# A planner that counts the overlap of VectorE and ScalarE instructions, and three more long score stretches

## The chip, the cores and the metric

One core of one Trainium2 chip. The metric is the time of one execution in device microseconds (us), lower is better; every median below comes with its range and number of runs. The span of a profile is 1.7 to 2.1 us shorter than the time of the same run; I compare spans with spans and times with times.

## The reference, cut to what matters

```python
def reference(q, k, v, w_gate, w1, w2):               # q, k, v: (4, 8, 768, 64)
    attn = _attn_ref(q, k, v)                         # window of +-15 keys, and 24 block summaries
    x = attn.transpose(0, 2, 1, 3).reshape(3072, 512)
    return _moe_ref(x, w_gate, w1, w2)                # 8 experts, 512 -> 1024 -> 512, Sinkhorn routing

# in _attn_ref: k_sum = max of k over blocks of 32 keys (summaries of keys)
#               scores = local scores (banded) and q . k_sum; one softmax over both
```

The kernel works on 16 "pairs" of heads (0 to 15). Expert 0 runs as filler work between the pairs, up to some 165 us; the other seven experts follow, and they fill TensorE (busy for 475.00 us of the 475 from 165 to 640 us).

## The kernel before

The kernel doesn't issue instructions in the order of its source. It adds *units* (an engine, a planned cost in us, what it depends on, the buffers it opens or uses) to a plan, and `Plan.order` simulates the engines greedily: it takes the unit that can start first, sets its planned start and end, and so on. The order that comes out is the order in which the kernel issues each engine's instructions. No time is measured in this; the planned costs are numbers in the source. One line in `order`:

```python
class Plan:
    HOP = 0.15                          # planned hand-over between engines
    ...
    def order(self):
        ...                             # t = when operands, buffers and the engine are free
            u.start, u.end, u.on = t, end, e
            free[e] = end               # the engine is free when the unit ends
```

```python
    X_BY_DMA = 12
    WHOLE = 10
    ...
        def key_max(i):                                  # a VectorE unit of one instruction
            nc.vector.tensor_reduce(out=ks[r][:, 0, 0:24], in_=kT[r][:]..., axis=AX.X, op=ALU.max)

        def key_max_split(i):                            # "the split": ksT, one small instruction
            nc.vector.tensor_tensor(out=ksT[r][:, 64:128]..., in0=ks[r][:]..., in1=own[:]..., op=ALU.mult)

        def summaries_2(i):                              # TensorE: ss needs ksT
            r, ss = i % NB, bank("a", "ss")
            for h in range(2):
                nc.tensor.matmul(ss[:, 0:HS], lhsT=ksT[r][:, 64 - 64 * h:192 - 64 * h], rhs=qT[r]..., ...)

        def block_out(i):                                # two instructions, the second reads the first
            nc.vector.tensor_tensor(out=dst..., in0=vs, in1=own_n..., op=ALU.mult)
            if i >= PB:
                nc.vector.tensor_copy(out=ve[0:64, 1:G, :], in_=ve[0:64, 0:1, :]...)

        def edges(i):                                    # four instructions
            for j in range(2):
                q0 = 64 + 32 * j
                nc.vector.tensor_tensor(out=ee[q0:q0 + 32, ...], in0=er[0:32, ...], in1=band[0:32, ...], op=ALU.mult)
                nc.vector.tensor_tensor(out=ee[q0:q0 + 32, ...], in0=er[96:128, ...], in1=band[96:128, ...], op=ALU.mult)

        def pair_whole(i, prio):                         # pairs 4 to 15
            ...
            bufs = [Buffer("s")] + (2 * [None] if i < WHOLE else [Buffer("a"), Buffer("a")])
            U["S", i, 0] = U["S", i, 1] = add("PE", 0.4 if i < WHOLE else 0.6, lambda: scores(i), deps, prio, ...)
            U["X", i, 0] = add("ACT", 0.97, lambda: score_exp(i, 0), [U["S", i, 0]], prio, uses=bufs[:1])
            if i < WHOLE:                                # two stretches of six score matmuls
                U["S", i, 1] = add("PE", 0.4, lambda: scores_1(i), deps, prio, opens=[buf])
            ...                                          # else one of twelve, in one double and two single banks
            U["ed", i] = add("DVE", 0.78, lambda: edges(i), ...)
            ...
        # block_out of pairs 4 to 15 is planned with 0.7
```

The softmax here doesn't subtract the row's maximum and nothing guards it: scores larger than these inputs give would overflow.

## Time and profile before

| kernel before | |
|---|---|
| time | 666.17 us, median of 3 (666.14 to 666.85); with the runs made beside the change 666.27, 6 runs (665.79 to 667.65) |
| span of the profile | 664.1 us (a run of 665.77 us), TensorE busy 99% |
| VectorE, ScalarE busy | 83%, 62% |
| excess on TensorE | 16.0 us, of which 7.7 between 20 and 165 us |

"Excess" is the time from one matmul's start to the next one's, less the median of its shape, summed. It shows waits that a list of idle times hides, because a matmul row lasts longer than the time to the next start (379 against 216 ns at 512 columns in the trace of before).

```profile
71.76 1.46 PE L211 MATMUL hps<-xT,w 128*128 128x384 f16 x8
73.06 0.49 PE L461 MATMUL ss<-qT,ksT 128*128 128x384 bf16 x2
```

The split ends at 72.22 + 0.21 = 72.43 and ss starts at 73.06, so 0.63 us of filler (hps) lie between. Over the twelve pairs 4 to 15 this distance is 0.35 us at the least: before the change TensorE never waited for a split.

### The profile page before, as it was taken

Reading aid. Unit: us, or ns where it says so; the run is one execution under the profiler, and the core shown is the slowest. Engines: PE = TensorE matmul, PEld = TensorE weight load, DVE = VectorE, ACT = ScalarE, POOL = GpSimd, SP = SyncE. Lnnn points to the kernel's source line nnn. Section 1 sums busy time; section 2 is a strip of 40 time slices with the busy share of each in tenths; the row PEclk is TensorE's granted clock in tenths of the full one; section 3 lists DMA queues with packets and bytes.
Section 4 is the critical chain, followed back from the end, with each engine's and each line's share of the span. In section 5 each row is a group of like instructions: output and inputs, shape, how many; then the busy total and the mean of one; then the engine's idle time right before and its main releaser. Section 6 shows DMA issues by size and latency. Waiting matters only on the chain.

```text
span 664.1 us, 13257 instructions
## 1 busy us (share of the span) xinstructions
PE 656.6 (99%) x5131; PEld 435.9 (66%) x5132; DVE 550.1 (83%) x1036; ACT 410.9 (62%) x769; POOL 199.0 (30%) x257
## 2 busy tenths in 40 slices
PE   8999999999999999999999999999999999999997
PEld 4666666545766666666666666666666666666666
DVE  7899897799988887887779877988778877988776
ACT  6677676556885566556665665555655656556652
POOL 8899522100132222212322222223122213222123
PEclk9999999999999999999999999999999999999999
DMA  9999932700953747373754665373838465335656
GB/s 167 181 145 145 143 70 43 128 1 2 157 96 65 126 75 118 64 128 65 110 97 71 121 91 101 64 127 65 127 64 135 73 96 96 64 64 112 157 134 202
DMA packets 112558, 67.89 MB, mean 102 GB/s; under 512 B 77936, under 2 KB 90480, under 8 KB 112496
## 3 DMA queue, kind: packets, MB, share of 16 engines
q0 software_dynamic: 94816, 57.46, 64.9%
q1 hardware_dynamic: 17152, 9.58, 5.9%
q8 instruction: 40, 0.66, 0.4%
q14 instruction: 22, 0.18, 0.1%
q10 hardware_dynamic: 528, 0.02, 0.0%
HBM read 52.45 MB, written 6.29 MB: 88 GB/s over the span
## 4 chain that ended last, share of the span: by engine, by line
PE 96%; DVE 3%; DMA 1%; issue 0%; ACT 0%; POOLq 0%; DVEq 0%
PE yps L815 22%; PE pA L764 22%; PE pY L815 17%; PE pQ L764 11%; PE hps L211 6%; PE yps L216 6%; PE pR L764 5%; PE sg L347 1%; DMA qst<-in_q_dram 1%; PE av L512 1%; PE vs L357 1%; PE tkq L303 1%; PE av L435 1%; DVE xs L543 1%; PE ss L461 1%; PE av L441 1%
## 5 line engine op out<-in xcount | busy, mean ns | idle before, releaser
L815 PEld LDWEIGHTS <-h 128*128 128x128 f16 x2352 | 230.1, 98 | 88.5 <-issue 1.0
L843 POOL DMA_DIRECT2D out_acc<-y x120 | 101.7, 891 | 372.1 <-ACT y L839 110.3
L839 ACT ACTIVATE y<-pY,P_sb 128x256 f32<-128x256 f32 x168 | 79.8, 477 | 123.3 <-PE pY L815 121.6
L830 DVE SCALAR_TENSOR_TENSOR out_acc<-yps,P_sb,out_acc 128x512 f32<-128x512 f32 x128 | 95.1, 744 | 29.0 <-PE yps L815 29.0
L798 DVE TENSOR_TENSOR h<-h 128x1024 f16<-128x1024 f16 x168 | 109.3, 683 | 1.4
L815 PE MATMUL pY<-w,h 128*128 128x256 f16 x672 | 100.0, 273 | 0.6 <-ACT y L839 0.6
L815 PE MATMUL yps<-w2sum,h 128*128 128x256 f16 x672 | 98.4, 273 | 0.0
L764 PE MATMUL pA<-xT,w 128*128 128x512 f16 x336 | 98.3, 379 | 0.0
L815 PE MATMUL yps<-w,h 128*128 128x256 f16 x672 | 93.3, 273 | 0.0
L830 DVE SCALAR_TENSOR_TENSOR out_acc<-pY,P_sb,out_acc 128x512 f32<-128x512 f32 x84 | 62.8, 748 | 29.1 <-PE pY L815 27.4
L764 PEld LDWEIGHTS <-w 128*128 128x128 f16 x672 | 65.8, 98 | 31.6 <-issue 0.2
L764 PEld LDWEIGHTS <-w1sum 128*128 128x128 f16 x504 | 49.3, 98 | 45.0
L786 DVE CUSTOM_DVE_ANT_0 h<-pQ,snap 128x512 f16<-128x512 f32 x84 | 57.6, 685 | 7.0 <-ACT snap L207 4.3
L786 DVE CUSTOM_DVE_ANT_0 h<-pA,snap 128x512 f16<-128x512 f32 x84 | 57.3, 682 | 4.8 <-PE pA L764 4.8
L202 ACT ACTIVATE h<-pA 128x512 f16<-128x512 f32 x84 | 50.6, 603 | 12.6 <-PE pA L764 12.4
L202 ACT ACTIVATE h<-pR 128x512 f16<-128x512 f32 x84 | 50.1, 596 | 8.0 <-PE pR L764 7.7
L207 ACT COPY pR<-pA 128x512 f32<-128x512 f32 x83 | 47.5, 572 | 7.7 <-PE pA L764 6.9
L815 PE MATMUL pY<-w2sum,h 128*128 128x256 f16 x336 | 50.4, 273 | 0.0
L764 PE MATMUL pA<-xsum,w 128*128 128x512 f16 x168 | 50.0, 379 | 0.0
L764 PE MATMUL pR<-xT,w 128*128 128x512 f16 x168 | 50.0, 379 | 0.0
L764 PE MATMUL pQ<-xsum,w1sum 128*128 128x512 f16 x168 | 50.0, 379 | 0.0
L764 PE MATMUL pA<-xsum,w1sum 128*128 128x512 f16 x168 | 50.0, 379 | 0.0
(150 smaller groups left out, 854.3 us busy)
## 6 DMA issues: line engine op xcount, KB each, us to landing
out_acc<-y POOLq DMA_DIRECT2D x120, 256.0 KB, 3.4
w<-in_moe_w_dram POOLq DMA_DIRECT2D x14, 1024.0 KB, 10.7
out_dram<-out_acc SPq DMA_DIRECT2D x24, 256.0 KB, 2.4
qst<-in_q_dram POOLq DMA_DIRECT2D x32, 96.0 KB, 5.3
vx<-in_v_dram POOLq DMA_DIRECT2D x15, 192.0 KB, 6.2
kst<-in_k_dram POOLq DMA_DIRECT2D x24, 96.0 KB, 5.6
w<-in_moe_w_dram POOLq DMA_DIRECT2D x4, 256.0 KB, 7.6
w<-in_moe_w_dram POOLq DMA_DIRECT2D x2, 512.0 KB, 7.7
```

The costliest lines, as they stand in the source:

```text
L202: nc.scalar.activation(out=out, in_=in_, func=AF.Relu, bias=0.0, scale=1.0)
L207: (nc.scalar.copy if eng == "ACT" else nc.vector.tensor_copy)(out=out, in_=in_)
L211: nc.tensor.matmul(hp[:, 0:n], lhsT=w1s[e][:, dk, f * 128:(f + 1) * 128], rhs=xT[:, dk, t0:t0 + n], start=(dk == 0), stop=(dk == KD - 1))
L216: nc.tensor.matmul(yp[:, d], lhsT=h[:, f, c * 128:(c + 1) * 128], rhs=w2s[e][:, f, d], start=(f == 0), stop=(f == KF - 1))
L303: nc.tensor.transpose(t[:, g * 128:(g + 1) * 128], st[:, g, :, :].rearrange("p j d -> p (j d)"), ident)
L764: nc.tensor.matmul(dst[:], lhsT=lhsT, rhs=rhs, start=first and k == 0, stop=k == HK - 1, skip_group_check=True)
L786: nc.vector._custom_dve(dve_ops.TENSOR_ADD_SAT, out=ring(e, p, q)[:, q % 2, blk, :], in0=at[src, e, p, q][:], in1=at.pop(("snap", n, e, p, ...
L798: nc.vector.tensor_tensor(out=h[:, :, out_, :], in0=h[:, :, a, :], in1=h[:, :, b, :], op=op)
L815: nc.tensor.matmul(dst[:, d], lhsT=lhsT, rhs=rhs, start=f == 0 and n in (1, 5, 2), stop=f == HF - 1, skip_group_check=True)
L830: nc.vector.scalar_tensor_tensor(out=o, in0=y, scalar=scalar, in1=o, op0=ALU.mult, op1=ALU.add)
L839: nc.scalar.activation(out=at[key][:, d], in_=src, func=AF.Copy, bias=0.0, scale=P_sb[:, t, e:e + 1])
L843: nc.gpsimd.dma_start(out=o, in_=at.pop(("y", e, p, c, key))[:], accum_op=ALU.add)
```

## The change

Intent: where work is queued, a VectorE or ScalarE instruction often begins a little before the one in front of it ends (in the trace of before by 82 and 103 ns in the median, where it does), so let the planner free the engine that much earlier; and let pairs 5, 7 and 9 too run their scores in one stretch over all six key chunks, as pairs 10 to 15 did, to save changes between matmuls of 128 rows and of 64. Making `X_BY_DMA` a set changes nothing (pairs 12, 13, 14 in both). The Sinkhorn rows' planned cost goes from 1.65 to 1.5. The diff, cut:

```diff
     HOP = 0.15
+    OVERLAP = {"DVE": 0.07, "ACT": 0.09}
...
-            free[e] = end
+            free[e] = end - self.OVERLAP.get(e, 0.0)
...
-    X_BY_DMA = 12
-    WHOLE = 10
+    X_BY_DMA = {12, 13, 14}
+    WHOLE = {5, 7, 9, 10, 11, 12, 13, 14, 15}
...
-            if i >= WHOLE:
+            if i in WHOLE:
...                                   (the other tests of WHOLE and X_BY_DMA likewise)
-            rows = add("DVE", 1.65, sink_rows, prev, 0)
+            rows = add("DVE", 1.5, sink_rows, prev, 0)
```

More of the change, by code (lines that the diff above doesn't have):

```diff
@@ L384, in scores @@
             dst = [[sg[:, j, :] for j in range(2)], None]
-            if i >= WHOLE:
+            if i in WHOLE:
                 dst[1] = at["sg", i, 1] = [bank("a", "sg1") for _ in range(2)]
-            score_mms(i, dst, range(G if i >= WHOLE else HG))
+            score_mms(i, dst, range(G if i in WHOLE else HG))
         def scores_1(i):
@@ L948, in pair_whole @@
             deps = [U["kT", i, 0], U["kT", i, 1], U.get(("ed", i - 2))]
-            bufs = [Buffer("s")] + (2 * [None] if i < WHOLE else [Buffer("a"), Buffer("a")])
-            U["S", i, 0] = U["S", i, 1] = add("PE", 0.4 if i < WHOLE else 0.6, lambda: scores(i), deps, prio,
+            bufs = [Buffer("s")] + (2 * [None] if i not in WHOLE else [Buffer("a"), Buffer("a")])
+            U["S", i, 0] = U["S", i, 1] = add("PE", 0.4 if i not in WHOLE else 0.6, lambda: scores(i), deps, prio,
                                               opens=[x for x in bufs if x is not None])
             U["X", i, 0] = add("ACT", 0.97, lambda: score_exp(i, 0), [U["S", i, 0]], prio, uses=bufs[:1])
-            if i < WHOLE:
+            if i not in WHOLE:
                 buf = Buffer("s")
@@ L978, in pair_whole @@
                                     [U["A", i, h], U.get(("x", i - 2))], prio, uses=[buf])
-            if i >= X_BY_DMA and i % PB < PB - 1:
+            if i in X_BY_DMA:
                 U["xt", i] = add("SP", 1.5, lambda: x_dma(i), [U["no", i, 0], U["no", i, 1]], prio)
@@ L1100, in transposed @@
             nc.gpsimd.tensor_copy(out=warm[:, 1:2], in_=qT[r][0:32, W:W + 1])
-            if X_BY_DMA < NP:
+            if NP - 2 in X_BY_DMA:
                 nc.gpsimd.tensor_copy(out=warm[:, 4:5], in_=xT[0:32, PB - 2, (B - 1) * S:(B - 1) * S + 1])
@@ L1108 @@
         last[0] = add("POOL", 0.3, transposed, [last[0], U["near", NP - 1]] + [U["kT", NP - 1, z] for z in range(2)]
-                      + [U["x", i] for i in range(X_BY_DMA, NP - 1)])
+                      + [U["x", i] for i in X_BY_DMA])
         load("w1n", lambda: load_w1(1), 0.85, 5.0)
```

## The prediction

> **What bounds the kernel now.** I read the page's first part, then stretches, then TensorE's waits, then single starts in the timeline. The page:
>
> ```profile
> PE 656.6 (99%) x5131; PEld 435.9 (66%) x5132; DVE 550.1 (83%) x1036; ACT 410.9 (62%) x769; POOL 199.0 (30%) x257
> PE 96%; DVE 3%; DMA 1%; issue 0%; ACT 0%; POOLq 0%; DVEq 0%
> ```
>
> TensorE (PE) is busy for 99% of 664.1 us and holds 96% of the chain that ended last. VectorE (83%) and ScalarE (62%) have room. The change alters how the order of VectorE and ScalarE is planned, so the first question is whether TensorE waits for them at all. The busy time of two stretches, and all TensorE waits above 150 ns that the view of waits lists:
>
> ```profile
> 20.00:165.00 145.00, 144.83 (x1421) 88.08 (x1419) 126.64 (x317) 97.57 (x174) 67.99 (x96) 1.00 1.11 93
> 165.00:640.00 475.00, 475.00 (x3292) 321.92 (x3291) 391.62 (x606) 294.27 (x564) 107.71 (x128) 1.00 0.57 98
> PE idle L613 <- DVE zeros L632: 1.3, 1, 1.3
> PE tkq L312 <- DMA qst<-in_q_dram: 0.8, 1, 0.8
> PE pY L815 <- ACT y L839: 0.6, 1, 0.6
> PE tkq L300 <- ACT kst L207: 0.3, 1, 0.3
> ```
>
> The stretch columns are width, then busy time and count of PE, PEld, DVE, ACT and POOL. From 165 to 640 us (the seven Strassen experts) TensorE is busy all the time. The waits are three in the first 7 us and one at 658 us.
>
> A busy matmul row can hide a short wait, because a row is longer than the gap between starts: a 512-column row lasts 379 ns, but the median start-to-start is 216 ns. So I compared each start-to-start time with the median of its shape (216, 162, 109, 56 ns for 512, 384, 256, 128 columns; for rare shapes columns at the same rate) and called the rest excess. It sums to 16.0 us: 7.1 us before 20 us (start-up[...]), 7.7 us from 20 to 165, less than 0.2 us from 165 to 640, and 1.0 us after 640. Only the 7.7 and the 1.0 can be won by scheduling.
>
> Most of the 7.7 us is no wait for an engine. It is 93 to 97 ns at each place where TensorE passes between matmuls of 128 rows and of 64 (or 32):
>
> ```profile
> 63.70 1.02 PE L216 MATMUL yps<-w,h 128*128 128x512 f16 x4
> 64.66 0.38 PE L347 MATMUL sg<-qT,kT 64*128 64x160 bf16 x6
> 64.97 0.51 PE L550 MATMUL tx<-ident_x,xs 128*128 128x128 f16 x6
> ...
> 90.10 1.03 PE L216 MATMUL yps<-w,h 128*128 128x512 f16 x4
> 91.06 0.59 PE L347 MATMUL sg<-qT,kT 64*128 64x160 bf16 x12
> 91.58 1.04 PE L216 MATMUL yps<-w,h 128*128 128x512 f16 x4
> ```
>
> Columns: start, length, engine, line. Four 512-column matmuls take 4 x 0.216 = 0.864 us, so the stream is free at 63.70 + 0.864 = 64.56, yet the scores (sg, 64 rows) start at 64.66: 0.096 us lost on entry. The exit costs 92 to 93 ns in the same reckoning. A stretch of six score matmuls thus costs 0.096 + 0.31 (64.66 to 64.97) = 0.41 us, one of twelve 0.096 + 0.52 (91.06 to 91.58) = 0.62 us. Waits for data in 20 to 165 us that I can name are two: 0.285 us (a transpose waits for a normalization at 20.6) and 0.21 us (logits wait for xT at 66.2).
>
> [...]
>
> ```profile
> 647.52 0.83 ACT L839 ACTIVATE y<-pY,P_sb 128x256 f32<-128x256 f32 x2
> 657.05 1.41 DVE L830 SCALAR_TENSOR_TENSOR out_acc<-yps,P_sb,out_acc 128x512 f32<-128x512 f32 x2 [0.63 <-PE yps L815]
> ```
>
> Two ACTIVATEs of 477 ns (mean row of their group) take 0.83 us, so they overlap by 0.12; two 744 ns VectorE rows take 1.41, an overlap of 0.08. Over the whole trace the median overlap, where one row begins before the previous ends, is 82 ns on VectorE (467 cases) and 103 ns on ScalarE (197). The planner's new constants, 0.07 and 0.09 us, are therefore close and still cautious.
>
> **The change part by part.** No matmul is added or removed: both built programs have 5,124 matmuls of the same shapes.
>
> 1. Pairs 5, 7 and 9: two stretches of six score matmuls become one of twelve. Counted in the built programs, the changes of row tiling fall from 86 to 80 (three entries, three exits). 6 x 94.5 ns = 0.57 us less on TensorE. Cross-check: 3 x (2 x 0.41 - 0.62) = 0.60 us. TensorE is on the path, so I take **-0.57 us** in full.
>
> 2. The second half's exponential of these pairs comes in two pieces of 480 elements: 1.04 us for two against 0.97 for one of 960 (rows of this trace), 3 x 0.07 = 0.2 us more on ScalarE, which is 67% busy there: off the path, 0. The pieces hold two of three shared PSUM banks instead of one double bank. That is the price that could turn into waits.
>
> 3. The overlap in the planner. It changes no duration, only order and who does what. By the count of built instructions ScalarE loses 13 copies of snap from pA and 9 from pQ, and 2 seeds of pR, all to VectorE: 24 x about 0.69 us = 16.6 us. Against 391.6 us in the 475 us stretch VectorE goes from 82% to 86%, ScalarE by 24 x 0.57 = 13.7 us from 62% to 59%. TensorE has no excess there to give back, so the gain is 0 and only a loss is possible. I put **+0.1 us** on it.
>
> 4. Order in the attention part (20 to 165 us). To see whether new waits are likely I laid out both orders with the start-to-start times above and read how much TensorE work lies between a producer and its consumer. Transpose of q to scores: 1.39 us at the tightest before, 0.91 (pair 4) and 1.29 after. The copy between needs 0.17 (end of the transposes) + 0.55 on VectorE or 0.80 on ScalarE + about 0.1: 0.82 or 1.07 us. So pair 4 may wait some 0 to 0.2 us. First to second scores of a pair: 1.72 before, 1.54 after; an exponential needs about 0.17 + 0.97 + 0.1 = 1.24. Values to transposes of x: 1.30 and 1.32. Last transposes of batch 0 to its logits: some 1.9 us of work, where 0.21 us was waited. I expect **-0.2 us** from the two old waits and **+0.2 us** for new ones.
>
> 5. The planned 1.5 us for the Sinkhorn rows (1.65 before) changes no instruction. In the trace the four take about 1.6 us (131.55 to 133.16) beside expert work: 0.
>
> 6. Order of DMA: POOL's issues stand as before; on SyncE the near values of pair 10 now go before the transposes of pair 12, and those of pair 13 before the near values of pair 11. The transposes landed at 73 to 76 us, the scores of pair 12 start near 91 (84 before): far apart.
>
> 7. The end. TensorE's last 24 matmuls, with the group that waits for y at 658, and VectorE's last 20 instructions stand as before: 0.
>
> Sum: -0.57 + 0.1 - 0.2 + 0.2 = -0.47 us; 666.17 - 0.47 = 665.7. Since the new planner's picture of the two engines is nearer to the trace, I lean slightly to fewer waits and say **665.5 us**.
>
> **The rivals.**
> - VectorE becomes late in the expert stage. For: 24 more copies[...]. Against: 86% busy on an overstated count (overlaps of 82 ns), and TensorE waited nowhere before. If every tenth of the 24 made TensorE wait 0.3 us: about +0.7 us, 666.3.
> - The two shared banks held by scores make transposes, values or block sums wait. For: three banks serve all of these. Against: pairs 10 to 15 already run so, with excess between 70 and 140 us of 1.7 us, nearly all of it tiling changes. One wait of 0.5 us a pair: +1.5 us, 667.2.
> - A finer plan packs TensorE truly tighter, removing all named waits, 0.5 us, and the 0.3 us near 645: 664.8. Against: the order around 645 is unchanged, and waits beside switches are few.
>
> **Range and chances.** The most that scheduling could win is 0.57 + 0.5 + 0.3 = 1.4 us (0.2%). A loss beyond 2% would be 13 us, nearly twice all excess of the attention part, with no mechanism for it. The three timed runs spread over 0.7 us. Range 664.5 to 667.0; within 2% is almost certain.
>
> **What would show it.** Right: score stretches on TensorE 23 instead of 26, each entry still about 96 ns; 165 to 640 us filled, with no TensorE wait in the view of waits there; VectorE's busy time up by some 12 us over the whole span and ScalarE's down by some 10 (the 24 copies less some relus and copies of the attention part that go the other way), with the end moved by under 1.5 us. Wrong: a new TensorE row on VectorE or ScalarE in the list of waits (snap, kT/qT copies, er), or a start in 20 to 165 us that has moved later than the switches explain.

(What the trace of before shows of the start: the first 512-column matmuls begin 401 to 427 ns apart, up to 4.2 us, against 216 later. The "about 0.1" of part 4 is an estimate for two hand-overs; between 20 and 165 us of that trace a ScalarE or VectorE row that waited for TensorE begins 37 or 38 ns after the end of the row it waited for, in the median, and a matmul that waited for VectorE begins 0.05 us after it in the trace of the change, below.)

## More of the kernel before

The next lines are from the timeline of the kernel before (start in us, length, engine, line, operation, output and inputs, count): first VectorE, then TensorE. They show the split of pair 9 (the sixth of the twelve, as in the plan's order) and the summaries that need it.

```profile
72.22 0.21 DVE L341 TENSOR_TENSOR ksT<-ks,own 128x64 bf16<-128x64 bf16 x1
```

## The result, and the profile after

667.37 us, median of 6 (667.24 to 669.93), against 666.27 of the kernel before in the same rounds. The ratio is 1.002, with a 95% interval of 1.0003 to 1.0037. (A ratio here is the mean time of one kernel's fast runs over that of the other's of the same rounds, so it is not quite the ratio of the medians; the one run of 669.93 pulls it up.) The time lies 0.37 us above the range: I had predicted a small gain, and it is a small loss of some 1.1 us.

The profile page of the changed kernel (its line numbers are one higher):

```profile
span 665.6 us, 13276 instructions
PE 657.5 (99%) x5131; PEld 435.5 (65%) x5132; DVE 563.9 (85%) x1053; ACT 403.1 (61%) x755; POOL 199.0 (30%) x257
PE 94%; DVE 4%; DMA 1%; issue 0%; ACT 0%; POOLq 0%; DVEq 0%
```

VectorE is busy for 13.8 us more and ScalarE for 7.8 us less, as predicted. On the chain that ended last, TensorE falls from 96% to 94% and VectorE rises from 3% to 4%. The two stretches:

```profile
20.00:165.00 145.00, 143.94 (x1412) 86.87 (x1411) 122.89 (x312) 98.98 (x181) 66.86 (x94) 1.00 1.12 93
165.00:640.00 475.00, 475.00 (x3290) 321.75 (x3289) 408.03 (x627) 283.89 (x540) 109.06 (x129) 1.00 0.57 98
```

The expert stretch is filled for all of its 475 us in both kernels, although VectorE has 16.4 us more to do in it: nothing is lost there. TensorE's busy time between 20 and 165 us fell by 0.89 us. The excess says the same: 16.0 us before, 17.5 after, and of the 1.5 us more all lie between 20 and 165 us (7.7 to 9.2), about 0.1 us in the expert stretch in both. The spans differ by 1.5 us too (664.1 and 665.6; the profiled run of before took 665.77 us, 0.5 below its median, so the 1.1 us of the medians is the safer size of the loss). So the place is settled before any experiment. In the list of TensorE's waits, which shows four as before (in all us, times, longest), one line is new:

```profile
...
PE ss L462 <- DVE ksT L342: 0.6, 2, 0.4
...
```

The summaries' matmul (ss) waits for the split (ksT). The other three are the start-up and the end, which were there before; the start-up wait for kst has left the list. By excess, the starts in 20 to 165 us that moved later beyond any tiling change are these:

| TensorE start, us | waits for | excess, ns |
|---|---|---|
| 67.88, 51.26, 86.38: ss | ksT (VectorE) | 594, 254, 270 |
| 84.12, 48.51: vs | VectorE xs; Ve | 278, 59 |
| 52.20: tkq; 47.33: av | VectorE xT | 260, 134 |
| 81.93: av | ScalarE kT | 158 |

(At 51.26 and 48.51 a change of tiling, 93 ns, is taken off already.) They sum to 2.0 us, and seven of the eight are for VectorE. How the largest arises, in the timeline of the changed kernel around 66 us (pair 9 again, VectorE and TensorE):

```profile
64.50 0.54 DVE L413 TENSOR_TENSOR em<-er,band 128x768 bf16<-128x768 bf16 x1
65.05 0.19 DVE L421 TENSOR_TENSOR Ee<-er,band 32x80 bf16<-32x80 bf16 x1
...
65.67 0.20 DVE L425 TENSOR_TENSOR Ee<-er,band 32x80 bf16<-32x80 bf16 x1
65.90 0.29 DVE L364 TENSOR_TENSOR Ve<-vs,own_n 64x128 bf16<-64x128 f32 x1
...
66.22 0.48 DVE L368 COPY Ve<-Ve 64x650 bf16<-64x650 bf16 x1
...
66.63 0.93 DVE L336 TENSOR_REDUCE ks<-kT 128x24 bf16<-128x768 bf16 x1
...
67.60 0.23 DVE L342 TENSOR_TENSOR ksT<-ks,own 128x64 bf16<-128x64 bf16 x1
...
67.88 0.50 PE L462 MATMUL ss<-qT,ksT 128*128 128x384 bf16 x2 [0.43 <-DVE ksT L342]
```

Read it on the VectorE rows. From the masks (em) to the split VectorE is never idle: masks 0.55, edges 0.85 (65.05 to 65.90), block_out 0.73 (65.90 to 66.63), key_max 0.97 (66.63 to 67.60), together 3.10 us. The plan gives these four, with the overlap taken off edges and block_out (edges needs the end of the masks and the split that of key_max, so there it doesn't count), 0.56 + 0.71 + 0.63 + 0.95 = 2.85. So the split comes 0.25 us late by these four alone, 0.14 of it in edges and 0.10 in block_out, and ss follows its end (67.60 + 0.23 = 67.83) by 0.05 us: it was waiting. Over pairs 4 to 15 the distance from the end of the split to ss, 0.35 us at the least before, is now about 0.06 at three of them, the three of the table.

**Theory A** is then: the overlap constants make the plan of VectorE too tight in the attention part. The planned costs of units of several instructions, edges above all, were always too short; the old planner, which counted no overlap at all, had room to spare elsewhere that covered it. The new one takes the cover away, places TensorE's consumers closer, and TensorE waits. What speaks for it without an experiment: the planner's own starts (which the program was made to print while being built) against the trace's, each counted from its own start. A trace doesn't name pairs; the splits are matched to the plan's by their order.

| split of pair 9 | planned start | start in the trace | trace less plan |
|---|---|---|---|
| before | 73.43 | 72.22 | -1.21 |
| change | 66.68 | 67.60 | +0.92 |

Over pairs 4 to 15 this difference is -0.32 to -1.47 us before, so the hardware runs ahead of the plan, and +0.10 to +1.35 after, behind it. Likewise the plan's end: 667.9 before (span 664.1), 666.1 after (span 665.6). The plan promised 1.8 us less; the hardware had been 3.8 us better than the old plan already.

And the units, from one start to the next where VectorE is back to back, in the trace of before, against the planned cost less 0.07: edges 0.86 against 0.71, block_out 0.72 against 0.63, sink rows 1.53 against 1.43; while masks (0.47 against 0.49), key_max (0.87 against 0.88), a normalization (0.69 against 0.68) fit.

The rivals: the banks that long stretches hold (the prediction's second rival), the new order of VectorE and ScalarE being worse by itself whatever its costs, the sink cost, and chance. In the expectations "A" is this theory; the other letters are rivals, and each text says with numbers what it expects of them.

### The profile page after: what moved, and what is told of

The parts are those of the page before. It is cut to its first block, busy times and chain, and to the rows that moved or that the text cites. A ratio compares the mean times of both kernels' runs of the same rounds, so it can differ in the third digit from the quotient of the medians.

```text
span 665.6 us, 13276 instructions
## 1 busy us (share of the span) xinstructions
PE 657.5 (99%) x5131; PEld 435.5 (65%) x5132; DVE 563.9 (85%) x1053; ACT 403.1 (61%) x755; POOL 199.0 (30%) x257
## 4 chain that ended last, share of the span: by engine, by line
PE 94%; DVE 4%; DMA 1%; issue 0%; ACT 0%; POOLq 0%; DVEq 0%
PE yps L816 22%; PE pA L765 22%; PE pY L816 17%; PE pQ L765 11%; PE hps L212 6%; PE yps L217 6%; PE pR L765 5%; PE sg L348 1%; DMA qst<-in_q_dram 1%; DVE ks L336 1%; DVE xs L544 1%; PE av L513 1%; PE tkq L304 1%; PE ss L462 1%; PE vs L358 1%; PE av L436 0%
## 5 line engine op out<-in xcount | busy, mean ns | idle before, releaser
L816 PE MATMUL yps<-w2sum,h 128*128 128x256 f16 x672 | 100.2, 273 | 0.0
L816 PE MATMUL yps<-w,h 128*128 128x256 f16 x672 | 90.5, 273 | 0.0
L765 PE MATMUL pQ<-xT,w1sum 128*128 128x512 f16 x168 | 50.0, 379 | 0.0
```

Of the source, the lines that this page charges most:

```text
L765: nc.tensor.matmul(dst[:], lhsT=lhsT, rhs=rhs, start=first and k == 0, stop=k == HK - 1, skip_group_check=True)
L816: nc.tensor.matmul(dst[:, d], lhsT=lhsT, rhs=rhs, start=f == 0 and n in (1, 5, 2), stop=f == HF - 1, skip_group_check=True)
```

## The experiments

All twelve were correct unless I say otherwise, timed with 5 rounds, in three calls; the kernel before had medians of 666.42, 666.21 and 666.12 us in them (9 runs each). Diffs are against the changed kernel unless they say otherwise.

### e1: the overlap alone

```diff
-    WHOLE = {5, 7, 9, 10, 11, 12, 13, 14, 15}
+    WHOLE = {10, 11, 12, 13, 14, 15}
-            rows = add("DVE", 1.5, sink_rows, prev, 0)
+            rows = add("DVE", 1.65, sink_rows, prev, 0)
```

> The overlap constants alone (pairs 5, 7 and 9 in two stretches as before, Sinkhorn rows planned at 1.65 as before). Theory A (the planner now takes 0.07 us off every VectorE unit, though edges and block_out were already planned shorter than the trace shows, so VectorE runs late and TensorE waits for ksT): about 1.2 to 1.7 us slower than before, VectorE again named in TensorE's waits (ksT, xs or xT), 86 changes of row tiling. Theory B (the shared banks held by the long score stretches make the waits): the same as before within 0.4 us. Theory C (any new order moves the time by about this much): anything within 1.5 us.

Measured: 667.35 us (666.68 to 668.64), ratio 1.0015 (1.0002 to 1.0027), excess 18.6 us. By the medians that is 0.93 us slower than before, under the 1.2 that A had expected, and about as much as the whole change loses; so the long stretches aren't needed for a loss, which weakens the rival of the banks (as do e3 and e15 below, whose traces keep the stretches and have no loss). But the waits aren't the same. TensorE's waits, and VectorE and TensorE in the timeline, of e1:

```profile
PE av L442 <- DVE Ee L421: 0.9, 1, 0.9
PE av L436 <- DVE em L413: 0.7, 1, 0.7
```

```profile
78.47 0.95 DVE L336 TENSOR_REDUCE ks<-kT 128x24 bf16<-128x768 bf16 x1 [2.64 <-DMA kT<-kst]
```

```profile
81.66 0.36 PE L436 MATMUL av<-vx,em 128*128 128x65 bf16 x6 [0.72 <-DVE em L413]
82.88 0.52 PE L442 MATMUL av<-Ve,Ee 128*128 128x130 bf16 x3 [0.87 <-DVE Ee L421]
```

Here the planner put the key_max of pair 12, whose kT comes by a DMA transpose, ahead of other work. VectorE stood for 2.64 us until the transpose landed, at 78.47; the masks and edges that stand behind key_max in the order began only at 81.05 and 82.22, and TensorE waited for them, 0.72 and 0.87 us. Up to pair 10 the splits of e1 were 0.0 to 0.5 us behind the plan, then 2.3 to 2.9. The run that was profiled is the slowest of the five, 668.64 us; whether the others, 666.68 to 667.61, wait as long for that transfer is not shown. So a tighter order can lose in two ways, the second seen in one run: by costs that are too short, and by a transfer that lands later than planned. e1 supports A in that the overlap is the cause, and not in how.

### e2: the long stretches alone

```diff
-    OVERLAP = {"DVE": 0.07, "ACT": 0.09}
+    OVERLAP = {}
-            rows = add("DVE", 1.5, sink_rows, prev, 0)
+            rows = add("DVE", 1.65, sink_rows, prev, 0)
```

> The long score stretches of pairs 5, 7 and 9 alone, planner without overlap. Theory A: 0.3 to 0.7 us faster than before (six changes of row tiling less, 0.57 us), no wait for ksT in TensorE's list. Theory B: 0.8 to 1.5 us slower than before.

Measured: 673.28 us (672.82 to 676.61), ratio 1.011 (1.0091 to 1.013): 6.9 us slower. A clean miss, for A and for B. TensorE in the timeline of e2:

```profile
54.41 0.50 PE L304 MATMUL tkq<-ident,kst 128*128 128x128 bf16 x6
54.74 0.50 PE L551 MATMUL tx<-ident_x,xs 128*128 128x128 f16 x6
...
56.62 1.89 PE L217 MATMUL yps<-w,h 128*128 128x512 f16 x8
...
60.13 0.34 PE L551 MATMUL tx<-ident_x,xs 128*128 128x128 f16 x3 [0.56 <-DVE xs L544]
...
61.67 0.50 PE L462 MATMUL ss<-qT,ksT 128*128 128x384 bf16 x2 [0.50 <-DVE ksT L342]
...
64.45 0.50 PE L304 MATMUL tkq<-ident,qst 128*128 128x128 bf16 x6 [0.65 <-DVE kT L208]
65.92 0.58 PE L348 MATMUL sg<-qT,kT 64*128 64x160 bf16 x6 [0.97 <-ACT qT L208]
...
70.65 0.84 PE L304 MATMUL tkq<-ident,qst 128*128 128x128 bf16 x6
71.29 0.84 PE L358 MATMUL vs<-vx,m_blk 128*128 128x128 bf16 x6
```

There is no filler (yps, hps) from 58.34 to 72.59 us: it had been spent earlier, and the next depends on values not yet made. Without filler the waits show, 0.50 to 0.97 us each in the lines above. The plan itself showed 5.2 us of idle TensorE, in gaps that begin between 60 and 70 us, which I had not looked at. And the clock is lower there: six transposes take 54.74 - 54.41 = 0.33 us from start to start, 55 ns each, and 71.29 - 70.65 = 0.64 us, 107 ns each, some 12 us after the last filler. The view of windows shows a granted clock of 0.93 from 62 to 66 us, where TensorE is busy for 1.76 us of the 4, 0.50 from 66 to 72 and 0.97 from 72 to 76; what sets it was not tested. By an estimate from these, 4 x 0.07 + 6 x 0.50 + 4 x 0.03 = 3.4 us of the 6.9 are clock. The mean clock of the timed runs is 0.990 to 0.995.

So the two parts of the change aren't independent: the long stretches of this very set pay only with an order that keeps filler for them.

### e13 and e14: which stretch empties the filler

Both with `OVERLAP = {}` and the sink cost 1.65; e13 has the long stretches of 7 and 9 and not of 5, e14 that of 5 alone:

```diff
-    OVERLAP = {"DVE": 0.07, "ACT": 0.09}
-    WHOLE = {5, 7, 9, 10, 11, 12, 13, 14, 15}
-            rows = add("DVE", 1.5, sink_rows, prev, 0)
+    OVERLAP = {}
+    WHOLE = {7, 9, 10, 11, 12, 13, 14, 15}       # e13; e14: {5, 10, 11, 12, 13, 14, 15}
+            rows = add("DVE", 1.65, sink_rows, prev, 0)
```

> Long score stretches for pairs 7 and 9 alone under the old planner. Theory F (the 7 us of the long stretches alone come from pair 5: in that order the expert matmuls that fill TensorE are used up by 58 us; the planner's own times show 5.2 us of idle TensorE there, against 1.35 us with 7 and 9 alone and 0.6 before): within 0.8 us of before, no wait over 0.9 us between 55 and 75 us. Rival B (any long stretch before pair 10 starves the shared banks): 3 to 5 us slower than before.

> The long stretch of pair 5 alone under the old planner. Theory F: 3 to 6 us slower than before, TensorE waits of several us together at 55 to 72 us with no expert matmul (hps, yps) between them, and a lower granted clock there. Rival B: 1 to 3 us slower, a third of what the three cost.

Measured: e13 666.11 us (665.88 to 667.32), ratio 1.0003 (0.999 to 1.0015), excess 15.7, with one wait for a split, 0.45 us at 65.5. e14 670.74 us (670.34 to 671.28), ratio 1.0067 (1.0054 to 1.0081). TensorE in the timeline of e14:

```profile
63.00 0.38 PE L348 MATMUL sg<-qT,kT 64*128 64x160 bf16 x6 [1.26 <-DVE qT L208]
...
64.49 0.38 PE L348 MATMUL sg<-qT,kT 64*128 64x160 bf16 x6 [0.68 <-ACT er L409]
```

No filler runs from 59.9 to 71.55 us, and the excess between 60 and 70 us is 5.4 us. Pair 5's long stretch under the old planner empties the filler; that is 4.6 of e2's 6.9 us. In e14 the clock costs less by the same estimate, 1.7 us (0.85 from 62 to 66 us, 0.50 from 66 to 68, 0.94 from 68 to 70), so most of the other 2.3 us is likely clock too; no run shows it. Pairs 7 and 9 alone do no harm, and gain at most what the noise hides. The one wait in e13 is for a split that starts 0.67 us ahead of its plan: TensorE there was further ahead still.

### e6: the sink cost alone

```diff
-    OVERLAP = {"DVE": 0.07, "ACT": 0.09}
-    WHOLE = {5, 7, 9, 10, 11, 12, 13, 14, 15}
+    OVERLAP = {}
+    WHOLE = {10, 11, 12, 13, 14, 15}
```

> Only the Sinkhorn rows planned at 1.50 instead of 1.65: a new order around the same durations. Theories A and B: the same as before within 0.4 us. Theory C: it moves by up to 1.5 us with no cause in the edit.

Measured: 666.19 us (666.13 to 666.53), ratio 0.9998 (0.9985 to 1.001). Nothing, as predicted in part 5. Built and compared, its order differs from that of before only from some 125 us on; so it is no test of the rival that any new order in the attention part moves the time.

### e3: the change with planned costs nearer to the trace

```diff
-            U["Vs", i] = add("DVE", 0.28 if i < PB else 0.7, lambda: block_out(i), [U["vs", i], sc],
+            U["Vs", i] = add("DVE", 0.28 if i < PB else 0.79, lambda: block_out(i), [U["vs", i], sc],
-            U["ed", i] = add("DVE", 0.78, lambda: edges(i),
+            U["ed", i] = add("DVE", 0.93, lambda: edges(i),
-            rows = add("DVE", 1.5, sink_rows, prev, 0)
+            rows = add("DVE", 1.6, sink_rows, prev, 0)
```

> The whole change, but edges planned at 0.93 (0.78), block_out at 0.79 (0.70) and the Sinkhorn rows at 1.60 (1.50), so that each less 0.07 is what the trace shows from start to next start (0.86, 0.72, 1.53). Theory A: the waits for ksT, xs and xT go, 0.2 to 0.9 us faster than before, 1.3 to 2.0 faster than the change. Theory B: as slow as the change, within 0.4 us of it. Theory C: anything within 1.5 us of before.

The three costs are those of the trace plus the 0.07 that the planner takes off: 0.86, 0.72 and 1.53 us. Measured: 665.48 us (665.38 to 665.70), ratio 0.9985 (0.9971 to 0.9999), excess 15.7 us, splits -0.27 to +0.52 us from the plan. Overlap, long stretches and banks are all still there; only planned costs differ, and the loss is gone. From the list of TensorE's waits in e3:

```profile
...
PE ss L462 <- DVE ksT L342: 0.2, 1, 0.2
...
```

One wait for a split is left, of 0.2 us in the list (0.33 by the excess of its start, at 49.5 us), where there were two with 0.6; the other lines of the list are start-up and end.

### e15: edges' cost alone, and e16: e3 once more

e15 is the changed kernel with one number changed; e16 is e3 again.

```diff
-            U["ed", i] = add("DVE", 0.78, lambda: edges(i),
+            U["ed", i] = add("DVE", 0.93, lambda: edges(i),
```

> The whole change with the planned cost of edges alone corrected (0.93 for 0.78). Theory A, with edges as its largest part (0.15 of 0.24 us a pair): 1.2 to 2.0 us faster than the change, within 0.4 us of the run with all three costs corrected. If block_out or the Sinkhorn rows matter as much: less than half of that.

> The run with all three costs corrected once more, on another chip and beside the two halves of the question: 0.5 to 1.3 us faster than before if the first finding holds; the same as before if it was the chip.

Measured: e15 665.24 us (664.97 to 665.73), ratio 0.9986 (0.9973 to 0.9999), excess 15.7 us: this one number takes the changed kernel's median down by 2.1 us (667.37 to 665.24, in different rounds; the intervals of the two ratios don't meet). The order changes with it, from some 46 us on; it shows that overlap, long stretches and banks need not lose, not what the cost does at one order. VectorE and TensorE in the timeline of e15, pair 9:

```profile
68.48 0.95 DVE L336 TENSOR_REDUCE ks<-kT 128x24 bf16<-128x768 bf16 x1
...
69.81 0.55 DVE L205 TENSOR_SCALAR h<-hps 128x384 f16<-128x384 f32 x1
70.28 0.21 DVE L342 TENSOR_TENSOR ksT<-ks,own 128x64 bf16<-128x64 bf16 x1
```

```profile
71.18 0.34 PE L442 MATMUL av<-Ve,Ee 128*128 128x130 bf16 x3
71.36 0.48 PE L462 MATMUL ss<-qT,ksT 128*128 128x384 bf16 x2
```

The split ends at 70.49, ss starts 0.87 us later and carries no wait. Planned for 70.09, the split starts 0.19 us behind the plan. (Those of pairs 4 to 6 are 0.8 to 1.2 us behind in this run, and TensorE waits for none of them.)

e16 does not simply repeat e3: 666.92 us, with five runs of 665.45, 666.92, 667.17, 665.38 and 667.29, ratio 1.0003 (0.9991 to 1.0016). Two runs lie at e3's level and three some 1.7 us higher, with clocks of 0.997 to 1.0 that don't sort them. e3 ran on another chip; e15 ran on e16's chip, and all its five runs are low. The profiled run was one of the low ones (span 663.7, excess 15.5), so no trace shows what the high ones wait for. Two things follow. That the corrected costs remove most of the waits for splits stands, in the traces of e3 and e15. That they make a kernel faster than the one before, by some 0.9 us, stands only at the edge of what can be told.

### e9, e10, e11: less and more VectorE time at the same order

Three kernels that leave the planned costs, and so the order, alone. e9 does only two of the four instructions of edges (a wrong result, relative error 0.025). e11 adds to the change a second copy of one instruction of edges, 0.21 us a pair, twelve times; e10 adds the same to the kernel before.

```diff
 # e9
-            for j in range(2):
+            for j in range(1):
 # e10 (against the kernel before) and e11 (against the change)
+                if j == 0:
+                    nc.vector.tensor_tensor(out=ee[q0:q0 + 32, 0:G - 1, 128 - W:128], ...)   # the first one again
```

> The change with its order untouched, but edges does two of its four VectorE instructions (0.42 us less for each of 12 pairs; wrong result on purpose). Theory A (VectorE is late against its plan: edges and block_out together take 0.24 us a pair more than planned): TensorE's waits for ksT, xs and xT between 45 and 90 us go, 0.8 to 1.6 us faster than the change, 0 to 0.8 faster than before. Theory B or D (the waits come from the shared banks or from where the score stretches stand): within 0.3 us of the change, since neither moves.

> The kernel before with one of the four edges instructions done twice (0.21 us more VectorE work for each of 12 pairs, 2.5 us in all; right result, same order). Theory A (the old plan left VectorE some 0.08 us of room in every unit, and the trace of before runs up to 1.5 us ahead of that plan): within 0.3 us of before. Rival (VectorE has no room in this stage in any order): 0.8 us slower or more.

> The same padding in the change. Theory A (its plan has no room left, the trace of the change runs up to 1.3 us behind it): 1.0 to 2.5 us slower than the change, 2 to 3.5 slower than before. Rival: as in the padded kernel before.

| | median us (range) | ratio to before (95%) |
|---|---|---|
| change | 667.37 (667.24 to 669.93) | 1.0020 (1.0003 to 1.0037) |
| e9, change with less | 666.46 (666.24 to 667.89) | 1.0007 (0.9994 to 1.0019) |
| e11, change with more | 668.79 (668.73 to 668.91) | 1.0037 (1.0025 to 1.005) |
| e10, before with more | 666.87 (666.50 to 667.15) | 1.0009 (0.9995 to 1.0022) |

At the order of the change, VectorE time costs both ways: 0.9 us less with edges halved, 1.4 us more with edges a quarter longer, and 1.4 is more than half of the 2.5 us that the twelve copies (12 x 0.21) take. The intervals of these ratios overlap with that of the change, so the times alone don't prove it; the traces do agree, with 0.9 us less and 1.4 us more excess. In e9 the wait for the split at pair 9 falls from 594 to 218 ns, that of the start near 51 us from 347 to 223 (93 of it the tiling change), the one near 86 us stays (272), and so do the wait for xT (262) and the one for kT (154). Of the 2.0 us in the table some 1.0 are left: about half of what A had expected to go has gone. e11's list has the same waits, longer (its line numbers are five higher here):

```profile
PE ss L467 <- DVE ksT L342: 0.8, 2, 0.7
...
PE vs L358 <- DVE xs L549: 0.3, 1, 0.3
...
```

At the order of before the same copies cost 0.66 us, where I had expected 0.3 at the most: a miss (the interval of the ratio takes in 1, but the excess of its trace grows by 0.8 us). The old order had less slack than I thought, though still half the price.

### e7: overlap and corrected costs, short stretches

e3 with `WHOLE = {10, ..., 15}`.

```diff
 # e3's three costs, and
-    WHOLE = {5, 7, 9, 10, 11, 12, 13, 14, 15}
+    WHOLE = {10, 11, 12, 13, 14, 15}
```

> Overlap constants and the three corrected costs, but pairs 5, 7 and 9 in two stretches as before. Theory A: no new VectorE waits, so 0.3 to 0.8 us slower than the run with the corrected costs and long stretches (six changes of row tiling more, 0.57 us), within 0.4 us of before. If the long stretches gain nothing: as fast as that run.

Measured: 666.76 us (665.93 to 667.11), ratio 1.0005 (0.9993 to 1.0018), excess 16.2 us. Against e3's 15.7 the long stretches are worth 0.44 us of excess (16.16 less 15.72), near the 0.57 predicted. The times don't show it: the median is 1.28 us above e3's and 0.55 above that of before, both outside what I had expected, the profiled run is the fastest of e7's five (665.93), and e16 shows that e3's kernel can be slower too.

## Why the prediction was wrong

- **Part 1, the tiling changes (-0.57 us): right.** Score stretches on TensorE are 23 after 26, and each entry still costs 95 to 97 ns. e7 and e3 show 0.44 us of it.
- **Part 3, overlap in the expert stretch (+0.1 us): right.** It is filled for 475.00 of 475 us, with VectorE up by 16.4 us (I had 16.6). The first rival named the right mechanism, VectorE late, in the wrong place.
- **Parts 2, 5, 6 and 7: zero, as said**, as far as runs show it: e6 for part 5; the wait at the end (pY for y, 0.6 us) is the same; only one new wait, of 0.16 us, is for ScalarE.
- **Part 4 failed: "I expect -0.2 us from the two old waits and +0.2 us for new ones."** Of the two old waits one went (0.21 us, logits for xT) and one stayed (near 20.7 us). The new waits are 2.0 us that I can name. Then -0.57 - 0.21 + 2.0 = 1.2 us of the 1.5 us by which excess and span grew; 0.3 us I cannot name. I had laid out the new order and checked four chains in it. The one that became the largest term, kT to key_max to split to summaries, I left out, because in the trace before nothing waits for it.
- **The reason under it: the sentence "the planner's new constants ... are therefore close and still cautious".** The median overlap of 82 ns was taken over pairs of rows that overlap, which says nothing on those that don't. Counted afterwards, between 20 and 165 us of the kernel before: of the rows of VectorE that follow within 60 ns, 124 overlap the one before (median 82 ns) and 164 do not; most of these begin 13 to 35 ns after its end. I had checked the constant, and not what it is subtracted from. (A recount over the whole trace of before finds 605 overlapping rows on VectorE and 319 on ScalarE for the prediction's 467 and 197, with the same medians; and 665.7 + 0.7 in its first rival is 666.4. Neither changes the argument.) Edges was 0.08 us too short even without it (0.86 against 0.78), and 0.15 with it.
- **"Since the new planner's picture of the two engines is nearer to the trace, I lean slightly to fewer waits"** was the lean in the wrong direction. The old picture erred in two ways that cancelled, too long between units and too short within some; the new one mends only the first.

What the experiments show: the loss goes when one planned cost is corrected (e15), without touching overlap, stretches or banks; and VectorE time at the change's order moves the excess, and the medians, both ways (e9, e11). What they don't settle: whether a reordering as such moves the end by half a microsecond or so (e1's other wait, e10's miss, e16's two levels say that it may), and why e16 has two levels. The best kernel measured is e15, some 0.9 us (0.14%) below the kernel before, at the edge of what can be told.

## What to carry to other kernels

A planner's constants are one set: correct one of them and you lose the cover it gave to the others, so before making a plan tighter hold the planned starts of whole units against the trace, and look at the drift. Its sign is a hint and no test: splits 0.8 to 1.2 us behind the plan did no harm in e15, and one 0.67 us ahead was waited for in e13; what counts is how late the engine is against the one that it feeds. When a statistic supports a constant, ask which cases it left out. And when an order changes, check every chain into the bounding engine, above all those where nothing waited before.

## What the traces show of the steps between instructions

- A change of row tiling on TensorE costs 91 to 98 ns at 74 of the 86 changes before; 9 of the others take 99 to 121 ns.
- On VectorE, between 20 and 165 us before, 124 of 288 back-to-back rows overlap the one in front, by 82 ns in the median; the other 164 don't, and most of them begin 13 to 35 ns after its end.
- All 36 steps within edges, whose inputs alternate between partitions 0 and 96, have gaps of 13 to 31 ns and no overlap, before and after. What makes these gaps is not shown: the copied instruction of e10 and e11 is the only step within edges with the same partitions, and it doesn't overlap either (34 to 35 ns of gap), but it rewrites what the one before it wrote.
- In block_out and the normalization the second instruction reads what the first wrote: 34 to 35 ns of gap in most cases (10 of 12 and 32 of 32 before).
